# A four-fold folded Fourier transform, and sums and gate products on a second elementwise engine, in a routed attention and long-convolution kernel

## The chip, the cores and the metric

The kernel runs on one core of a Trainium2 chip. The metric is device time in microseconds (us), the median over several executions (a program can also run some per cent slower at a lower clock). "Span" is the length of the one execution that was profiled, which lies about 2 us under the time of the same run. The engines are TensorE (PE in the views, PEld its weight loads), VectorE (DVE), ScalarE (ACT), GpSimd (POOL) and SyncE (SP), which here only issues DMAs; SPq is its queue.

## The reference

```python
def attn(q, k, v, centroids):            # batch 4, 8 heads, 768 rows, 64 columns; 16 centroids a head
    q_assign = argmax(normalised(q) . normalised(centroids))      # likewise k_assign
    mask = q_assign[..., :, None] == k_assign[..., None, :]
    scores = where(mask, q @ k.T / sqrt(64), -1e9)
    p = exp(scores - max);  return (p / (sum(p) + 1e-9)) @ v

def mixer(x, w_proj, filter_fft, w_out): # x: 4 x 768 x 512
    x1, x2, x3 = split(x @ w_proj)
    conv = irfft(rfft(x2) * rfft(filter_fft))      # along the 768 rows
    return (x1 * conv * x3) @ w_out
```

The output of the attention is the input of the mixer. All is float32 outside; inside, scores, spectra and projections are in bfloat16.

## The kernel before

The program is written as some 1,900 small operations, each with the engines that may run it, a duration that the program assumes, and a due time. A planner in the kernel simulates the core at build time with these durations and so fixes the order of every engine's queue. A list of due-time corrections, `NUDGE`, and a dozen settings were tuned so that this plan becomes short.

```python
def op(self, eng, fn, due, r=(), w=(), ...):
    o.eng = eng                        # {"engine": assumed duration in us}
    o.due += NUDGE.get(o.seq, 0.0)     # e.g. {10:3.7, 75:-1.5, 90:7.4, ...}
...
op(("DVE", 1.75), acc, ...)            # probability sum, 128 x 1536
```

The attention takes 96 calls of `pv` (probabilities times values) on TensorE, twelve to a group of four heads; between them stand the scores, the routing of the next group and the mixer of the last finished batch. The spectrum of the mixer is a product with a cosine and sine table `fw`. The rows are first folded once: the sum and the difference of row blocks that mirror each other. So three pairs of products make a spectrum:

```python
def spectrum(ps, i, cs):
    for m in range(3):
        if i < 2:
            columns(ps, T.fw[:, i, m, 192*cs:192*cs+128], T.uv2[:, i, m], m == 0, m == 2)
        ...
```

The spectral sums and the gate products (`y1 * x3`) run on VectorE, save four sums of the last batch.

The softmax here doesn't subtract the row's maximum and nothing guards it: scores larger than these inputs give would overflow.

## Time and profile before

| | kernel before |
|---|---|
| time, median | 389.92 us (388.98 to 390.6, 4 runs) |
| span | 388.5 us |
| TensorE, VectorE, ScalarE, GpSimd busy | 369.0, 359.0, 269.8, 47.0 us |
| first and last `pv` call | start 25.5, end 342.3 us |
| where the plan made at build time ends | 381.2 us |

The prediction below shows the page, the chain and the windows. One view matters besides: what TensorE waits for in its fixed order. Between the 36th and the 96th call (131.3 to 342.3 us) the list of waits has seven rows, 3.1 us in sum, and these lead it. After each pair of waiter and releaser stand us in total, times, and the longest.

```profile
PE bank L73 <- DVE x L871: 0.9, 1, 0.9
PE bank L73 <- DMA aug<-ohT: 0.7, 1, 0.7
```

Waits on VectorE's results make 2.4 of the 3.1 us, masks (`aug<-ohT`) 0.7. The two engines are both almost full, and the order that was found for them makes neither wait for the other.

### The profile page before, as it was taken

To read this page: it belongs to the slowest core of one execution; us is meant where nothing else is said; L and a number is where in the kernel's file an instruction comes from. 1 tells how busy PE (TensorE), PEld (TensorE's weight loads), DVE (VectorE), ACT (ScalarE), POOL (GpSimd) and SP (SyncE) were. 2 spreads that over 40 slices of the span, in tenths; PEclk is the share of its full clock that TensorE was granted. 3 is DMA by queue.
4 is the path that set the end of the run, shared out by engine and by line. 5 is a ranking of instruction groups with operands and counts; after the bars stand their busy time and mean duration, and the time that the engine had idled before them with its cause. 6 is when DMAs were issued, how large, how long until landed. Compare 5 with 4: busy or idle time off the path is not lost.

```text
span 388.5 us, 8482 instructions
## 1 busy us (share of the span) xinstructions
PE 369.0 (95%) x3256; PEld 214.3 (55%) x3256; DVE 359.0 (92%) x509; ACT 269.8 (69%) x514; POOL 47.0 (12%) x92
## 2 busy tenths in 40 slices
PE   2999998999999999999999999999999999999995
PEld 1564454444445555555455554665454566557893
DVE  8898998899899999999899999999999999999782
ACT  5898687887884878787865976778865567632342
POOL 8502000000021010101010100101010100000400
PEclk9999999999999999999999999999999999999999
DMA  9819973740769759966897695745645651110214
GB/s 179 190 52 221 213 165 80 167 120 20 166 134 153 138 83 172 112 144 85 160 136 198 71 275 100 140 88 70 133 60 172 73 161 12 43 43 2 92 74 162
DMA packets 93860, 47.17 MB, mean 121 GB/s; under 512 B 82088, under 2 KB 87676, under 8 KB 93820
## 3 DMA queue, kind: packets, MB, share of 16 engines
q1 hardware_dynamic: 87836, 36.84, 41.6%
q0 software_dynamic: 2704, 8.98, 16.6%
q10 hardware_dynamic: 3280, 0.82, 1.2%
q8 instruction: 25, 0.41, 0.5%
q14 instruction: 15, 0.12, 0.1%
HBM read 31.59 MB, written 7.40 MB: 100 GB/s over the span
## 4 chain that ended last, share of the span: by engine, by line
PE 47%; DVE 35%; issue 7%; ACT 5%; DMA 3%; SPq 0%; DVEq 0%; POOL 0%; ACTq 0%; POOLq 0%
PE bank L73 17%; DVE acc L695 14%; PE pair L681 14%; PE bank L807 5%; PE bank L71 4%; DMA rb<-dr 2%; DVE oh L607 2%; PE bank L555 2%; DVE aug L262 2%; ACT p L670 2%; DVE tm L831 1%; PE bank L584 1%; DVE x L871 1%; ACT aug L260 1%; DVE mx L605 1%
## 5 line engine op out<-in xcount | busy, mean ns | idle before, releaser
L681 PE MATMUL pair<-p,vraw 128*64 128x385 f32 x768 | 142.9, 490 | 0.0
L670 ACT ACTIVATE p<-bank 128x512 f32<-128x512 f32 x192 | 113.7, 610 | 34.8 <-PE bank L73 33.3
L695 DVE TENSOR_TENSOR acc<-p,acc 128x1536 f32<-128x1536 f32 x64 | 111.9, 1749 | 3.5 <-ACT p L670 1.3
L681 PEld LDWEIGHTS pair<-p,vraw 128*64 128x64 f32 x768 | 54.0, 136 | 49.8 <-issue 45.2
L73 PE MATMUL bank<-aug,aug 80*64 80x512 bf16 (+3 forms) x590 | 69.7, 327 | 3.4 <-DVE den L717 1.0
L667 ACT ACTIVATE p<-bank 128x512 f32<-128x512 f32 x96 | 58.6, 610 | 2.7 <-PE bank L73 1.5
L73 PEld LDWEIGHTS <-aug 80*64 80x64 bf16 (+1 forms) x590 | 34.9, 109 | 34.7 <-issue 22.6
L729 POOL DMA_DIRECT2D acc<-acc x30 | 24.0, 799 | 245.5 <-DVE acc L695 85.4
L73 PE MATMUL bank<-xT,wpj 128*64 128x384 bf16 x424 | 41.4, 326 | 0.0
L260 ACT COPY qkT<-bank 128x384 f32<-128x384 f32 x62 | 27.9, 496 | 13.7 <-PE bank L73 8.9
L73 PEld LDWEIGHTS <-wpj 128*64 128x64 bf16 x424 | 27.9, 109 | 12.5 <-issue 6.7
L73 PEld LDWEIGHTS <-y 128*64 128x64 bf16 x448 | 24.9, 110 | 9.1 <-issue 3.0
L695 DVE TENSOR_TENSOR acc<-p,p 128x1536 f32<-128x1536 f32 x16 | 28.0, 1750 | 2.0 <-ACT p L670 2.0
L831 DVE TENSOR_TENSOR tm<-bank,hm 128x512 f32<-128x512 f32 x44 | 27.6, 677 | 0.8 <-ACT p L670 0.5
L260 ACT CAST aug<-qkT 64x768 bf16<-64x768 f32 x29 | 24.0, 829 | 3.0 <-PE bank L73 2.6
L807 PE MATMUL bank<-wpj,xT 128*64 128x512 bf16 x192 | 21.8, 380 | 0.4 <-DVE xT L775 0.4
L73 PE MATMUL bank<-wout,y 128*64 128x512 bf16 x176 | 21.4, 379 | 0.2 <-DVE y L909 0.2
L71 PE MATMUL bank<-aug,aug 80*128 80x256 bf16 (+3 forms) x89 | 19.9, 321 | 0.7 <-DVE tm L831 0.4
L555 PE MATMUL bank<-ident,qkraw 128*128 128x128 f32 x144 | 19.8, 279 | 0.2 <-DVE oh L607 0.2
L555 PEld LDWEIGHTS bank<-ident,qkraw 128*128 128x128 f32 x144 | 15.6, 140 | 7.1 <-issue 5.3
L260 ACT COPY tm<-bank 128x512 f32<-128x512 f32 x14 | 8.1, 590 | 16.1 <-PE bank L807 11.6
L262 DVE CAST aug<-qkT 64x768 bf16<-64x768 f32 x31 | 17.5, 569 | 1.5 <-PE bank L73 0.9
(149 smaller groups left out, 440.6 us busy)
## 6 DMA issues: line engine op xcount, KB each, us to landing
vraw<-in_v_dram SPq DMA_DIRECT2D x16, 384.0 KB, 4.3
qkraw<-in_q_dram SPq DMA_DIRECT2D x30, 192.0 KB, 5.0
qkraw<-in_k_dram SPq DMA_DIRECT2D x30, 192.0 KB, 5.1
rb<-dr SPq DMA_DIRECT2D x30, 192.0 KB, 3.7
out_dram<-ob SPq DMA_DIRECT2D x11, 512.0 KB, 3.6
acc<-acc POOLq DMA_DIRECT2D x10, 384.0 KB, 4.8
acc<-acc POOLq DMA_DIRECT2D x10, 192.0 KB, 4.0
y<-in_moe_filter_fft_dram SPq DMA_DIRECT2D x4, 384.0 KB, 6.8
```

The source lines that it names most:

```text
L71: return T.nc.tensor.matmul(out, lhsT, rhs, start=start, stop=stop)
L73: T.nc.tensor.matmul(out[64 * i:64 * i + 64], lhsT[:, 64 * i:64 * i + 64], rhs, start=start, stop=stop)
L260: T.nc.scalar.copy(out, in_)
L262: (T.nc.vector if e == "DVE" else T.nc.gpsimd).tensor_copy(out, in_)
L555: T.nc.tensor.transpose(bank(h.ids[i // 3])[:, ts(i % 3, 128)], raw(s, i), T.ident)
L667: T.nc.scalar.activation(o, ap(h).rearrange("p (a b) -> p a b", a=2), Act.Exp, scale=0.125)
L670: T.nc.scalar.activation(flat(s)[:, lo:lo + 512], ap(h), Act.Exp, scale=0.125)
L681: T.nc.tensor.matmul(o[64 * hp:64 * hp + 64, ch, :385], T.vraw[vs][:, hp, sk * D:(sk + 1) * D], T.p[slots[sk]][:, hp, 384 * ch:384 * ch + ...
L695: T.nc.vector.tensor_tensor(T.acc[os], P_(t[0]), P_(t[1]) if len(t) == 2 else T.acc[os], op=Alu.add)
L729: op(("POOL", .8), lambda e, rows=rows: T.nc.gpsimd.dma_start(flat_()[:rows], flat_()[rows:2 * rows], accum_op=Alu.add), te, r=[], w=[("ac ...
L807: T.nc.tensor.matmul(ap(h)[64 * i:64 * i + 64], T.xT[xs][:, kt, c:c + 64], T.wpj[:, kt, DM:2 * DM], start=kt == 0, stop=kt == ND - 1)
L831: op(("DVE", .68), lambda e, i=i, cs=cs, r=r, h=h: T.nc.vector.tensor_tensor(T.tm[r][:, cs], ap(h), hmrow(i, (0, 2, 2, 3)[2 * r + cs]), op ...
```

## The change

It folds the rows once more, so that a spectrum takes two pairs of products; two additions over 1024 columns per batch (`quarters`) make the folded rows on VectorE, and half of the query columns are stored in mirrored order so that the rows come out in place. GpSimd may now run the spectral sums and the gate products of all batches but the last. The last batch's gates no longer wait in the inverse's order. The filter comes in 12 transfers of 128 KB, three fp32 products with a flipped identity matrix mirror it, and all settings and the list were fitted anew.

```diff
 def spectrum(ps, i, cs):
-    for m in range(3):
+    for m in range(2):
+        slot = lambda e: T.uv2[:, 4 + (e + cs) % 2 if m else 2 * e + cs]
...
+def quarters(due):
+    for o_, out in ((Alu.add, slice(0, 4, 3)), (Alu.subtract, slice(1, 3))):
+        op(("DVE", 1.2), lambda e, ...: T.nc.vector.tensor_tensor(T.uv2[:, out], T.tm[0], T.tm[1], op=o_), ...)
...
-    op({"POOL": 1.45, "DVE": .68} if last and i < 2 else ("DVE", .68), ...               # spectral sums
+    op({"POOL": 1.45, "DVE": .68} if last and i < 2 or not last else ("DVE", .68), ...
-    op(("DVE", .95), ...                                                                  # gate products
+    op({"DVE": .95, "POOL": 2.2} if not last else ("DVE", .95), ...
-    g = op(("PE", .648), G, ..., after=gs[-1:] + (inv[dt-2:dt-1] if dt > 1 else []))
+    g = op(("PE", .648), G, ..., after=[] if last else gs[-1:] + (inv[dt-2:dt-1] if dt > 1 else []))
...
-LEAD = 1.97516      BUSY = 8.32578      b0 = end - 24.00965      w0 = A(24 * (b + 1)) + 11.85069
+LEAD = 21.93933     BUSY = 20.94041     b0 = end - 40.78980      w0 = A(24 * (b + 1)) + 44.32403
-NUDGE = {10:3.7,75:-1.5,90:7.4, ...}                   # and the other settings
+NUDGE = {2:0.3,3:0.6,5:-0.1, ...}
```

(The settings, one to a line in the program, are gathered here.)

## The prediction

> **What bounds the kernel now.** I read the page first, parts 1 and 2.
>
> ```profile
> PE 369.0 (95%) x3256; PEld 214.3 (55%) x3256; DVE 359.0 (92%) x509; ACT 269.8 (69%) x514; POOL 47.0 (12%) x92
> ...
> PE   2999998999999999999999999999999999999995
> PEld 1564454444445555555455554665454566557893
> DVE  8898998899899999999899999999999999999782
> ```
>
> Two engines look full, so busy time alone does not say which one sets the end. Matmul ends are modelled, so I rebuilt TensorE's work from the chain of waits, where calls stand back to back.
>
> ```profile
> 134.60 1.45 PE pair L681 x8
> 136.04 0.65 PE bank L450 x6
> 136.69 1.30 PE pair L681 x8
> 137.99 0.65 PE bank L450 x6
> ```
>
> One attention-value call (8 instructions) is 1.30 us, or 1.45 just after a change of array shape; a spectrum call of three pairs of 64-row matmuls over 512 columns is 0.65, so 0.217 a pair. In the same view twelve fp32 transposes took 1.46 us, sixteen similarity matmuls 1.43, forty-eight 512-column matmuls 5.23. With these unit costs and the program's order of instructions (0.13 us for each of 82 shape changes) TensorE's work is 363 us: 13 before the first attention-value call, 308 from there to the last, 41 after. The windows cut at those calls:
>
> ```profile
> 0.00:25.50 25.50, 17.43 (x130) 10.93 (x130) 22.21 (x52) 19.20 (x38) 14.46 (x52) 1.00 0.74 156
> 25.50:342.10 316.60, 310.04 (x2623) 169.56 (x2622) 300.94 (x399) 235.10 (x447) 27.54 (x36) 1.00 0.65 125
> 342.10:388.50 46.40, 41.56 (x509) 33.83 (x505) 35.83 (x60) 15.51 (x30) 5.01 (x4) 0.99 0.21 78
> ```
>
> After each length come PE, PEld, DVE, ACT and POOL. The middle holds 308 us of TensorE work in 316.6 us: 8.6 us is all that TensorE loses to anybody in 96 key tiles. VectorE is busy 301 of the 316.6. So TensorE bounds the middle, with VectorE close behind. The start loses 12 us (25.5 less 13), mostly before any data or VectorE's first tables are ready.
>
> The last part I read in the timeline. The last channel mixer starts its 48 projection matmuls at 348.75. Its VectorE work then runs almost without a gap from the first line below until the inverse starts:
>
> ```profile
> 352.95 3.67 DVE L820 TENSOR_TENSOR uv<-tm,bank 128x512 bf16<-128x512 f32 x6
> ...
> 358.97 2.50 POOL L835 TENSOR_TENSOR y<-tm 128x512 bf16<-128x512 f32 x2 [49.60 <-DVE tm L831]
> ...
> 360.28 2.52 DVE L831 TENSOR_TENSOR tm<-bank,hm 128x512 f32<-128x512 f32 x4 [0.27 <-POOL y L835]
> ...
> 368.19 0.72 PE L73 MATMUL bank<-inv,y 128*64 128x192 bf16 x12
> ```
>
> TensorE is kept busy meanwhile with gates and with the third batch's output product, but it is the VectorE chain that releases the inverse at 368.19.
>
> **What the Trainium skill says.** "TensorE: Matmul & The Clock Gate", Back-to-back issue gap, gives 518 cycles for 512 columns, 216 ns; this trace agrees (0.217 a pair). "Perfetto Trace Analysis", Identifying the Most-Contended Engine, says matmul busy share is no good measure of the distance to the roofline; hence the work sum. "GPSIMD Engine Reference", Elementwise side-by-side, has GpSimd about 1.96 times slower on a two-input operation; here the spectral sum is 1272 ns against 676, or 1.88. "SBUF — State Buffer", Who interferes with whom, says that VectorE with two SBUF inputs contends with a GpSimd instruction that reads SBUF, and that one is blocked outright; with one SBUF input it does not. The trace shows both sides: a one-column operation of VectorE took 0.78 us instead of 0.16 and ended when GpSimd's cast did, while the four PSUM-fed products above (360.28) ran at 0.63 each beside two GpSimd sums.
>
> ```profile
> 8.46 0.16 DVE L318 TENSOR_TENSOR s<-s,ss 128x1 f32<-128x1 f32 x1
> ...
> 8.60 0.82 POOL L262 CAST aug<-qkT 64x768 bf16<-64x768 f32 x1
> 8.65 0.78 DVE L319 TENSOR_TENSOR s<-s,s 128x1 f32<-128x1 f32 x1
> ```
>
> **The change, part by part.** The rows of groups that I cost with:
>
> ```profile
> L831 DVE TENSOR_TENSOR tm<-bank,hm 128x512 f32<-128x512 f32 x44 | 27.6, 677 | 0.8 <-ACT p L670 0.5 <-POOL y L835 0.3
> L835 DVE TENSOR_TENSOR y<-tm 128x512 bf16<-128x512 f32 x20 | 13.0, 676 | 0.0
> L909 DVE TENSOR_TENSOR y<-yy,x 128x768 bf16<-128x768 f32 x12 | 11.5, 958 | 0.5
> L835 POOL TENSOR_TENSOR y<-tm 128x512 bf16<-128x512 f32 x4 | 5.0, 1272 | 49.8 <-DVE tm L831 49.8
> L262 DVE CAST aug<-qkT 64x768 bf16<-64x768 f32 x31 | 17.5, 569 | 1.5 <-PE bank L73 0.9
> ```
>
> *TensorE.* Each of 30 spectrum calls (6 in the tables, 24 in the batches) goes from three pairs to two: 30 x 0.217 = 6.5 us removed. Fewer table transposes: 0.4. Added: three fp32 matmuls with the flip matrix; an fp32 pair of 385 columns is 0.325 x 2, so 512 columns are 0.86 each, 2.6 us. Shape changes go from 82 to 78 (0.5). Net -4.8, to 358. By place: -2.9 up to the last attention-value call, -1.9 after it (1.3 of it spectra, the rest a gate call that moves ahead).
>
> *VectorE.* The instruction orders of both kernels count: 17 spectral sums go to GpSimd (17 x 0.676 = 11.5), 9 gate products too (9 x 0.958 = 8.6), 11 casts go to ScalarE (6.3), two table adds of 1536 columns (3.5), one of three angle chains (2.7) and some copies (2.2) vanish. Added: two quarter butterflies over 1024 columns per batch, 1.21 each between the 677 ns of 512 columns and the 1749 of 1536: 9.7; ten table butterflies, 6.8; ten evictions taken from ScalarE, 5.5, and a small copy. Net -12.6, to 346. In the last batch, though, the butterflies are +2.4 in the chain that releases the inverse.
>
> *GpSimd.* +17 x 1.272 = 21.6, and 9 products over 768 columns, estimated from 1272 ns at 1.9 us each: 17. It ends near 85 us. Where VectorE's next instruction has two SBUF inputs, as the 1.75 us sum of the probabilities has, it waits. At an estimated 0.3 to 0.5 us for each of 26 moves, 8 to 13 us of VectorE's gain is handed back, as waiting or longer instructions. *ScalarE* gains some 6 us; with 69% busy that costs nothing.
>
> **What lies on the path.** Middle: TensorE -2.9. VectorE's relief lies beside it and can only cut into the 8.6 us of stalls; the port waits and GpSimd's queue, where sums stand behind the accumulating DMAs, add some. I take -0.5 net. Start: with one angle chain fewer, VectorE's centroid part and so the first scores come earlier; I take -1.5 of 2.7. End: TensorE has 1.9 less to do, but the inverse waits for VectorE. Its work from the first butterfly to the last sum was 15.2 us; it becomes about 18 (quarters +2.4, more gate products ahead of the inverse +1.5, the rest -1), and TensorE's fill is 5.2 + 10.4 + 2.6 + 3.5 = 21.7 us with all gates ahead of the inverse against 19.4 before. After the inverse's start four gate products fewer stand in the way. The two nearly cancel: -0.8. Sum: -2.9 - 0.5 - 1.5 - 0.8 = -5.7, and 389.7 becomes 384.0.
>
> **Rivals.** (a) VectorE was the real bound, and its 12.6 us count nearly in full: for it, the long stretches of probability sums in the chain of waits (35% VectorE); against it, only 8.6 us of stall in the middle. That gives about 379. (b) The port lock and the queue behind the DMAs eat the relief, and VectorE becomes the bound with some 355 us and new gaps; TensorE's saving turns to idle time. For it: the blocked operation above and 26 moves onto an engine that was idle; against it: the sums are followed mostly by PSUM-fed products. That gives 386 to 390. (c) The end grows, since the butterflies lengthen its only chain: +1 to +2 there, so about 386.
>
> **Range and chances.** Faster by over 2% means under 381.9, which needs at least 2 us of the stalls gone besides all that I counted: 0.27. The schedule's many tuned priorities could give that, or take it. Slower by over 2% would need over 12 us of new waiting (7.8 and the 4.8 saved), more than the middle loses now: 0.03. Range 379.5 to 388.0.
>
> **What would show it.** Right: TensorE's busy time near 364, VectorE's at 346 to 352 with probability sums or table adds that last over 1.75 us beside GpSimd's sums; the last attention-value call 4 to 6 us earlier than 342; the distance from the last projection's start to the end about unchanged at 39.7. Wrong: a first attention-value call still at 25.5; stalls in the middle well under 8.6 (rival a), or VectorE waiting for GpSimd by more than 5 us in sum (b); a longer end (c).

## More of the kernel before

The filter comes in four transfers of 384 KB, and the routing of each group ends in a transposing DMA from SyncE, followed by eight small transfers (the masks) into the operands of the scores:

```python
op(("SP", .6), lambda e: T.nc.sync.dma_start_transpose(T.ohT..., T.oh...), due - 2, r=both("oh"), ...)
masks(n, range(2), due + 1.3)
```

## The result, and the profile after

The changed kernel takes **406.14 us** (403.88 to 408.92, 4 runs), against 389.92. Ratios here and below compare fast runs of the same rounds, so they are not quite the ratio of the medians quoted. This one is 1.0421, with a 95% interval of 1.0352 to 1.049. The kernel is slower by 4%, where the prediction had it 1.5% faster. The page of the changed kernel, parts 1 and 2:

```profile
PE 370.7 (92%) x3274; PEld 214.6 (53%) x3274; DVE 361.9 (89%) x491; ACT 276.9 (68%) x518; POOL 90.3 (22%) x117
...
PE   3999189999999998999898999999898999999995
...
DVE  8789639899899789999997899999999999999981
```

VectorE does as much as before (359.0), although 26 operations went to GpSimd. In the fifth of the forty slices, at 40 to 50 us, TensorE stands almost still. The windows, cut at the first and last `pv` call, show that the loss lies between the two:

```profile
26.18:359.00 332.82, 311.58 (x2646) 174.61 (x2647) 305.62 (x381) 241.96 (x451) 69.86 (x61) 0.98 0.61 119
359.00:404.70 45.70, 39.98 (x499) 27.32 (x495) 35.24 (x58) 15.80 (x30) 6.86 (x5) 0.99 0.21 79
```

The middle grew from 316.6 to 332.8 us; the end hardly moved (46.4 to 45.7).

To find where in the middle, I added up TensorE's work in program order with the unit costs of the prediction and took it from the time at which every twelfth `pv` call ended. What is left is TensorE's lost time so far. (The last two columns are experiments, told below.)

| `pv` calls | before | changed | filters in a row | planned anew |
|---|---|---|---|---|
| 12 | 14.2 | 24.1 | 13.6 | 12.8 |
| 36 | 17.0 | 24.5 | 14.0 | 13.6 |
| 48 | 18.1 | 29.6 | 19.2 | 15.0 |
| 60 | 19.3 | 34.0 | 24.3 | 17.5 |
| 96 | 20.8 | 40.4 | 30.7 | 18.5 |
| end | 25.8 | 46.8 | 37.2 | 24.4 |

There are two losses: some 10 us before the twelfth call, and from the 36th call on some 16 us where the kernel before loses 4. The end costs both kernels 5 to 6.5.

**The first loss.** SyncE's queue in the changed kernel (start, length, operation, output<-input, count; timeline):

```profile
27.07 6.34 SPq L388 DMA_DIRECT2D y<-in_moe_filter_fft_dram  x10
36.96 1.53 SPq L659 DMA_TRANSPOSE ohT<-oh  x1
38.54 1.26 SPq L388 DMA_DIRECT2D y<-in_moe_filter_fft_dram  x2
```

Ten of the twelve filter transfers go out, then a transposing DMA stands in the queue until VectorE has finished the routing it reads, at 36.9 us. The other two filter transfers stand behind it. Meanwhile GpSimd, whose guard waits for one filter piece alone, has started the 2 MB of weights at 35.5 us. The two late pieces, 128 KB each, land at 51.5 us, and TensorE waits for them:

```profile
51.66 2.04 PE L432 MATMUL bank<-y,xT 128*128 128x512 f32 x2 [7.49 <-DMA y<-in_moe_filter_fft_dram]
```

The wait is 7.5 us of the loss. Some 2 us more come after it, as the windows around it show; after the busy times stand the clock that was granted to TensorE (1.00 is full speed), the DMA share and GB/s:

```profile
44.00:51.00 7.00, 0.17 (x1) 0.00 (x0) 2.73 (x5) 0.00 (x0) 0.00 (x0) 0.85 1.17 199
51.00:55.00 4.00, 3.34 (x11) 0.85 (x11) 1.25 (x3) 0.60 (x1) 0.00 (x0) 0.50 1.05 233
55.00:57.00 2.00, 2.00 (x14) 0.74 (x12) 1.70 (x2) 0.49 (x1) 0.00 (x0) 0.82 0.12 39
57.00:61.00 4.00, 4.00 (x38) 2.06 (x35) 1.09 (x2) 2.68 (x5) 0.00 (x0) 1.00 0.74 169
```

The two matmuls above took 2.04 us at half the clock; in e2 below, where TensorE does not stand still, the same two took 1.02. The estimate from these windows is 3.34 x 0.5 + 2.00 x 0.18, or 2 us.

**VectorE's lengthening.** The durations (least, median, largest, in ns) of the large sums of VectorE in the kernel before, then in the changed one, where the next two lines are GpSimd's sums and products:

```profile
L695 DVE TENSOR_TENSOR acc<-p,acc x64: 1694/1752/1759, 28.7 to 342.0; 128x1536 f32<-128x1536 f32 x64
```

```profile
L727 DVE TENSOR_TENSOR acc<-p,acc x64: 1695/1757/3520, 30.1 to 359.1; 128x1536 f32<-128x1536 f32 x64
...
L869 POOL TENSOR_TENSOR y<-tm x21: 1262/1273/2716, 163.8 to 382.5; 128x512 bf16<-128x512 f32 x21
L944 POOL TENSOR_TENSOR y<-yy,x x9: 1815/1819/3180, 189.5 to 362.0; 128x768 bf16<-128x768 f32 x9
```

The medians agree, the largest do not: some instructions were held for most of another one's length, on either side. From the groups' means, the lengthening on VectorE is 64 x (1813 - 1749) = 4.1 us for these, 16 x (1938 - 1750) = 3.0 for the other large sums, 10 x (642 - 173) = 4.7 for an operation over 12 columns, and 15 x (1165 - 1006) = 2.4 for the normalised output: 14.2 us.

### The profile page after: what moved, and what is told of

The parts are those of the page before. It is cut to its first block, busy times and chain, and to the rows that moved or that the text cites. A ratio compares the mean times of both kernels' runs of the same rounds, so it can differ in the third digit from the quotient of the medians.

```text
span 404.7 us, 8563 instructions
## 1 busy us (share of the span) xinstructions
PE 370.7 (92%) x3274; PEld 214.6 (53%) x3274; DVE 361.9 (89%) x491; ACT 276.9 (68%) x518; POOL 90.3 (22%) x117
## 4 chain that ended last, share of the span: by engine, by line
PE 45%; DVE 25%; DMA 9%; ACT 8%; issue 7%; SPq 4%; ACTq 0%; DVEq 0%; POOL 0%; POOLq 0%
PE bank L74 18%; PE pair L713 13%; DVE acc L727 6%; SPq L492 3%; DMA y<-in_moe_filter_fft_dram 3%; PE bank L839 3%; ACT aug L267 2%; ACT p L702 2%; DVE oh L639 2%; DMA ohT<-oh 2%; DMA rb<-dr 2%; DVE tm L865 2%; PE bank L72 1%; PE bank L586 1%; DVE xT L807 1%
## 5 line engine op out<-in xcount | busy, mean ns | idle before, releaser
L702 ACT ACTIVATE p<-bank 128x512 f32<-128x512 f32 x192 | 113.0, 609 | 37.4 <-PE bank L74 24.3
L727 DVE TENSOR_TENSOR acc<-p,acc 128x1536 f32<-128x1536 f32 x64 | 116.1, 1813 | 3.4 <-ACT p L702 1.2
L74 PE MATMUL bank<-aug,aug 80*64 80x512 bf16 (+3 forms) x616 | 73.4, 329 | 6.0 <-DMA aug<-ohT 1.6
L74 PE MATMUL bank<-xT,wpj 128*64 128x384 bf16 x488 | 46.9, 326 | 0.4 <-DVE oh L639 0.4
L869 POOL TENSOR_TENSOR y<-tm 128x512 bf16<-128x512 f32 x21 | 31.9, 1527 | 39.5 <-DVE tm L865 25.0
L74 PEld LDWEIGHTS <-wpj 128*64 128x64 bf16 x488 | 31.9, 109 | 14.5 <-issue 7.1
L267 ACT CAST aug<-qkT 64x768 bf16<-64x768 f32 x41 | 33.6, 829 | 2.3 <-DVE qkT L269 1.0
L727 DVE TENSOR_TENSOR acc<-p,p 128x1536 f32<-128x1536 f32 x16 | 31.0, 1938 | 1.5 <-DMA dd<-acc 0.9
L944 POOL TENSOR_TENSOR y<-yy,x 128x768 bf16<-128x768 f32 x9 | 18.3, 2032 | 35.5 <-DVE yy L941 27.1
L586 PE MATMUL bank<-ident,qkraw 128*128 128x128 f32 x144 | 19.2, 279 | 0.3 <-DVE x L906 0.3
L267 ACT COPY ob<-bank 128x512 f32<-128x512 f32 x22 | 12.7, 589 | 9.5 <-PE bank L74 9.0
L72 PE MATMUL bank<-aug,aug 128*128 128x256 bf16 (+3 forms) x76 | 16.8, 321 | 1.5 <-DMA aug<-ohT 0.7
## 6 DMA issues: line engine op xcount, KB each, us to landing
vraw<-in_v_dram SPq DMA_DIRECT2D x16, 384.0 KB, 4.2
acc<-acc POOLq DMA_DIRECT2D x10, 384.0 KB, 5.1
```

The source lines that it names most:

```text
L72: return T.nc.tensor.matmul(out, lhsT, rhs, start=start, stop=stop)
L74: T.nc.tensor.matmul(out[64 * i:64 * i + 64], lhsT[:, 64 * i:64 * i + 64], rhs, start=start, stop=stop)
L267: T.nc.scalar.copy(out, in_)
L586: T.nc.tensor.transpose(bank(h.ids[i // 3])[:, ts(i % 3, 128)], raw(s, i), T.ident)
L702: T.nc.scalar.activation(flat(s)[:, lo:lo + 512], ap(h), Act.Exp, scale=0.125)
L727: T.nc.vector.tensor_tensor(T.acc[os], P_(t[0]), P_(t[1]) if len(t) == 2 else T.acc[os], op=Alu.add)
```

## The experiments

All kernels are correct unless stated, and every ratio is to the kernel before in the same rounds.

**Theories at the start.** A: the filter loads behind the transposing DMA cost the first 9 to 10 us. B: GpSimd's sums and products cost the rest. C: the fitted settings, above all `LEAD`, which lets loads go out early, cost the rest.

### e1: the twelve filter loads in a row

```diff
+    first = min(order.index(o) for o in T.early)       # T.early: the twelve filter loads
+    order = [o for o in order[:first] if o not in T.early] + T.early + [o for o in order[first:] if o not in T.early]
```

> Theory A (a filter load stuck in a queue): in the changed kernel the last two of twelve filter loads stand on SyncE's queue behind a transposing DMA that waits for VectorE until 36.96; they then share the DMA engines with 2 MB of weights and land only at 51.5, while TensorE waits in order at the third flip product. With the twelve loads issued in a row, all else in the same order, the wait of 7.5 us goes and the time falls by 8 to 11 us from 406 to about 396. Rival (the stall only covers waits that would come later anyway, since VectorE and the masks are late): under 3 us, 403 or more.

Measured: 397.11 us, ratio 1.0155 (1.0108 to 1.0203). That is 9.0 us below the changed kernel, and theory A is shown. The second loss is all there, as the table shows (14.0 at call 36, 30.7 at call 96). From here on e1 is the base.

### e2: the weights held until the last filter piece

```diff
-        op(("POOL", .1), lambda e: T.nc.gpsimd.tensor_copy(T.wpj[0:1, :, 0:1], T.f[1][0:1, 0, 0:4]...), 29,
+        def gate(e):
+            for r in (0, 64):
+                T.nc.gpsimd.tensor_copy(T.wpj[r:r + 1, :, 0:1], T.f[1][r:r + 1, 2, 0:4]...)
+        op(("POOL", .1), gate, 29,
```

> Order of the queues as in the changed kernel, but the 2 MB of weight loads start only when the last filter piece has landed. If it is the sharing with the weights that stretches the two late loads to 12.3 us (theory A2), they land in about 3 to 5 us after their issue at 38.5 and the time falls by some 6 to 8 us, to about 399. If the place in SyncE's queue alone is to blame (rival), they still land late and the time stays within 2 us of 406.

Measured: 398.76 us, ratio 1.0197. With the queue as it was, keeping the weights back takes 7.4 us from the changed kernel's time. In the trace the whole first loss is gone: TensorE waits for no filter piece, and its 36th `pv` call ends at 122.0 us, in e1 at 122.2. So the first loss is two small transfers sharing the way with 2 MB; their late issue alone costs nothing that can be seen. The 1.6 us by which e2 trails e1 are within the noise (give or take 2.8 us, from the intervals of the two ratios), and in the traces they arise after call 36, where the waits for masks, explained under e9, sum to 5.7 us against 4.2.

### e3: the sums and products back on VectorE

```diff
+    for o in T.moved:          # the 17 sums and 9 products of batches 0 to 2 (e1 as the base)
+        o.on = "DVE"
```

> As e1_filter_first, but the 17 spectral sums and 9 gate products that went to GpSimd run on VectorE again, at the same place in the program's order. Theory B (GpSimd gives back what it takes): VectorE's instructions with two SBUF inputs [...] lost about 14 us to longer durations in the changed kernel (sums of probabilities 1813 and 1938 ns against 1749, the small column operation 642 against 173, the scaled copy to xT 1165 against 1006), while 20 us of work left it, so moving back changes VectorE's busy time by only +4 to +7 and the time by -3 to +4 us against e1. Rival 1 (GpSimd was a clear gain): slower than e1 by over 5 us. Rival 2 (GpSimd is the main loss): faster than e1 by over 4 us.

Measured: 398.67 us, ratio 1.0193, 1.6 us above e1. The lengthening is gone:

```profile
L727 DVE TENSOR_TENSOR acc<-p,acc x64: 1696/1757/1761, 28.6 to 350.9; 128x1536 f32<-128x1536 f32 x64
```

VectorE's busy time is 365.2 us against 361.6. Moving 26 operations to GpSimd takes some 20 us from VectorE and gives most of it back as held instructions; the net is 3.6 us of VectorE. The 1.6 us of time are not clear of noise (give or take 2.6). Theory B falls, as undoing the move does not make e1 faster: in this order the move is not what costs.

### e4: the old LEAD

```diff
-LEAD = 21.93933
+LEAD = 1.97516        # e1 as the base
```

> As e1_filter_first, but the lead of loads (how long before its due time a load may be issued) is 1.98 again instead of 21.94, and the scheduler plans anew. Theory C (early loads of q, k and v crowd the queue and the DMA engines in front of the routing masks, whose transposing DMA landed in a median of 13.2 us instead of 2.8): the masks land in 3 to 6 us again and the time falls by another 3 to 6 us below e1, to about 391. Rival (the long lead is not what delays the masks, and the other tuned priorities fit the long lead): no gain, within 2 us of e1 or slower.

Measured: 406.08 us, ratio 1.039, 9 us slower than e1. Theory C in this form falls, but the run says little more: the planner makes a wholly new order with a list that was fitted to the other setting, and its own plan ends at 389.4 us, 10.8 later than with the new `LEAD`.

### e5 to e8: what the mixed stage is worth to each engine

e5 makes the quarter additions short. Its output is wrong, which doesn't matter for the time.

```diff
-T.nc.vector.tensor_tensor(T.uv2[:, out], T.tm[0], T.tm[1], op=o_)
+T.nc.vector.tensor_tensor(T.uv2[:, out, :16], T.tm[0][:, :, :16], T.tm[1][:, :, :16], op=o_)
```

> Wrong on purpose (not correct): with the filter loads in a row as in e1_filter_first, and each of the eight quarter additions (1222 ns each on VectorE in the changed kernel) over 16 of its 512 columns. It takes about 8 x 1.2 = 9 us of work from VectorE, alone, and leaves TensorE, GpSimd and every order as they are. Theory D (VectorE sets the pace of the mixed stage, from call 36 of the 96 attention-value calls on): 6 to 9 us below e1 (397.1), 388 to 391. Rival E (TensorE's work or the late routing masks set it): no more than 2 us below e1.

e6b gives TensorE its third pair back, once thrown away.

```diff
-        for m in range(2):
+        for m, first, final in ((0, True, True), (0, True, False), (1, False, True)):
```

> The result stays right: e1 with the first pair of products of each of the 30 spectrum calls issued twice (once thrown away), which gives TensorE back the third pair that the change took out: 30 x 0.217 = 6.5 us, 24 of them in the mixed stage (5.2). Theory D: TensorE has slack there, so at most 2 us above e1. Rival E (TensorE bounds it, as the prediction had it): 5 to 6.5 us above e1.

Measured, page part 1 of e5 and then of e6b:

```profile
PE 365.1 (94%) x3274; PEld 209.0 (54%) x3274; DVE 353.7 (91%) x491; ACT 276.7 (71%) x518; POOL 90.1 (23%) x117
```

```profile
PE 372.5 (93%) x3334; PEld 214.5 (54%) x3334; DVE 362.1 (91%) x491; ACT 276.5 (69%) x518; POOL 89.9 (23%) x117
```

e5 took 394.91 us, ratio 1.0071 (1.0004 to 1.0139): with 7.9 us of VectorE less (361.6 to 353.7), 0.0084 of 390, or 3.3 us, are won, give or take 3.2. e6b took 399.49 us, ratio 1.0206 (1.0147 to 1.0265): with 6.2 us of TensorE more, 0.0051 of 390, or 2.0 us, are lost, give or take 3.0. e5 lies between what the two theories expected, e6b at the upper edge of theory D. What can be said is that in this order neither engine's work counts one to one; the shares, two fifths and a third, are rough.

One thing moves between these runs that no edit aimed at: TensorE's waits for masks sum to 4.2 us in e1's profiled run, 5.5 in e3's, 1.6 in e5's (391.59 us, the fastest of its four by 3 us) and 3.9 in e6b's, with SyncE's queue in the same order. A difference of 1 or 2 us between two of them is therefore not to be read as the effect of the edit.

e7 moves the query, key and value loads near a transposing DMA behind its masks:

```diff
+    for tr, ms in T.routes:       # a transposing DMA and its eight masks
+        late = [loads within 6 us before tr, or between tr and the last mask]
+        order = [... all but late, up to the last mask ...] + late + [... the rest ...]
```

> e1 with the loads of query, key and value that stand in SyncE's queue just before or between a transposing DMA of the routing and its mask transfers moved behind the masks; nothing else moves. Theory F (late masks, held up by queue and bandwidth, cost a part of the mixed stage): the attention-value calls 36 to 60 come 3 to 6 us earlier and the end with them. Rival (VectorE holds the stage anyway, theory D): within 1 us of e1.

Measured: 402.83 us, ratio 1.0297, slower than e1. What the edit aimed at came: the transposing DMA that in e1 is issued at 113.0 us, and followed by its first mask 8.5 us later, is here followed by it after 2.8. But TensorE now waited 5.0 us in two waits for copies of queries and keys that came late. The edit was too coarse, and it leaves theory F open.

e8 chains the last gates again:

```diff
-  after=[] if last else gs[-1:] + (inv[dt - 2:dt - 1] if dt > 1 else []))
+  after=gs[-1:] + (inv[dt - 2:dt - 1] if dt > 1 else []))
```

> e1 with the last batch's gates chained in the inverse's order again, as in the kernel before; only the orders of TensorE and VectorE in the last projection, transform and output differ. The prediction gave this part 0.8 us. If it was right, 0.5 to 1.5 us above e1; the stretch from the start of the last projection to the end, 39.8 us in before and in the changed kernel, suggests within 0.5 us.

Measured: 397.78 us, ratio 1.0148 beside e1's 1.0155. The ratios put it 0.3 us below e1, give or take 3.2, the medians 0.7 above; that cannot tell nothing from the predicted 0.8. In the profiled runs (e8's is its slowest) the stretch from the start of the last projection to the end of the last matmul is 36.2 us here and 35.3 in e1, and to the end of the span 43.0 and 40.0. So what the separated gates are worth stays open.

### e9: masks that wait for nothing

e1's list of TensorE's waits between the 36th and the 96th call (122.2 to 349.3 us) sums to 12.5 us, where that of the kernel before had 3.1. Its first five rows:

```profile
PE bank L74 <- DMA aug<-ohT: 2.6, 2, 1.5
PE bank L74 <- DVE x L906: 1.7, 4, 0.8
PE bank L72 <- DMA aug<-ohT: 1.6, 1, 1.6
PE bank L74 <- DVE uv L853: 1.5, 2, 1.2
PE bank L74 <- DVE tm L865: 1.5, 4, 0.7
```

Late masks make 4.2 us, and results of VectorE, spread over nine rows, 8.3. For e9 the transposing DMAs are taken from the order, and the masks copy old rows. Its output is wrong, which doesn't matter for the time.

```diff
+    order = [o for o in order if o not in T.gone]           # the seven transposing DMAs
-    rows = slice(64*j + 2*pr + hp, 64*j + 64, 4) if n else slice(64*pr + 32*j + 16*hp, ...)
+    rows = slice(64 + 32*j + 16*hp, 64 + 32*j + 16*hp + 16)
```

> Wrong on purpose: e1 with the seven transposing DMAs of the routing taken out of the emitted order and every mask transfer reading rows that the first batch wrote. Orders of all engines stay, only SyncE's queue loses the seven. In e1, TensorE waited 4.2 us for routing masks between call 36 and call 96 and 8.3 us for results of VectorE. Theory F (the masks cost what is waited for them): 3 to 5 us below e1 (397.1), 392 to 394. Theory D (VectorE holds the mixed stage): the wait moves to VectorE's results, at most 2 us below e1. Either way the waits on masks must be gone from the trace.

Measured: 393.09 us, ratio 1.0069; no wait on masks is left in the list. Theory F holds for its part: of the 6 us by which e1 trails the kernel before, about 3.4 (0.0086 of 390, give or take 2.1) are masks. The transposing DMA that e1 issues at 113.0 us, with loads of queries, keys and values around it in the queue, is followed by its first mask after 8.5 us; in the kernel before none takes more than 5.4. e7 shows that these loads delay it (2.8 us without them). That the large `LEAD` is what put them there was not shown.

### e10 and e11: both kernels without their fitted lists

```diff
-NUDGE = {...}
+NUDGE = {}
```

> The kernel before with its list of hand-fitted priorities emptied, everything else its own. At build time its planner then plans an end at 395.8 us (381.2 with the list; the chip took 389.9, 8.7 more). Theory G (the plan's durations are nearly right for the kernel before, whatever the order): 403 to 407 us, that is 7 to 11 above its plan. Rival H (the gap to the plan is an accident of one order): gap anywhere from 5 to 25.

> e1 with its list of priorities emptied, its other settings kept. Its planner plans 386.1 us (378.6 with the list; e1 took 397.1 on the chip, 18.5 more). Theory G (the changed kernel runs further behind any plan, because GpSimd's additions lengthen VectorE's, which the plan does not know, and its masks land later than planned): 402 to 408, 16 to 22 above its plan, so no faster than the kernel before without its list. Rival H (the extra 10 us are an accident of e1's one fitted order): 394 to 397, 8 to 11 above its plan, and clearly faster than the kernel before without its list.

Measured: before without its list 404.05 us (ratio 1.0353), changed with the filters in a row and without its list 397.13 (1.0161). Without lists the changed kernel is 7 us faster. The two should not be read as a clean measure of the change: the kernel before without its list loses only after the last `pv` call, which ends at 342.0 us there and at 342.3 with the list. But the gap to the plan tells something. Times are the medians:

| kernel | plan ends | measured | gap | VectorE too short in the plan |
|---|---|---|---|---|
| before | 381.2 | 389.9 | 8.7 | 22.8 |
| before, no list (e10) | 395.8 | 404.1 | 8.3 | 23.3 |
| changed, filters in a row (e1) | 378.6 | 397.1 | 18.5 | 34.9 |
| the same, old `LEAD` (e4) | 389.4 | 406.1 | 16.7 | 28.2 |
| the same, no list (e11) | 386.1 | 397.1 | 11.0 | 27.5 |
| changed, planned anew (e12) | 382.5 | 384.5 | 2.0 | 7.7 |
| before, planned anew (e13) | 381.2 | 388.5 | 7.3 | 13.2 |

The last column is the busy time of VectorE in the trace less what the planner of that kernel counts for it (it can be run again from the kernel's file). The gap grows with it by and large, but the plan of the kernel before, too, had VectorE 23 us too short and was off by only 8.7.

The list of the kernel before is worth 14.6 us in the plan and 14.1 on the chip. The changed kernel's is worth 7.5 in the plan and nothing on the chip. Theory G was too pessimistic (11.0 against 16 to 22), and rival H, that this one fitted order is at fault, holds for the larger part.

### e12: the changed kernel planned with measured durations

The plan gives VectorE 326.7 us of work; the trace shows 361.6. To see what this does, I kept e1's order on every engine and computed its times again with durations from e1's trace. All of them together (large sums 1.836 us for 1.75, the two row-sum instructions 1.1 for 0.5, the marking of the largest similarity 1.02 for 0.55, the normalised output 1.17 for 1.05, and a longer transposing DMA, which is an allowance and not a measured size) move the end by 17.0 us, to 395.6. The measured span is 395.1. Taken alone, the transposing DMA moves it most, by some 8 us, then the marking and the large sums. The same for the kernel before, with its own two wrong durations, ends at 387.7; its span is 388.5. This is a calculation, made after the fact, and no run. The run that follows from it puts these durations into the planner and searches the list and the settings anew (by random changes kept if the plan gets shorter, 45 minutes):

```diff
-  op(("DVE", 1.75), acc, ...          op(("DVE", .5), gather, ...       op(("DVE", .55), ... Alu.is_equal
+  op(("DVE", 1.83), acc, ...          op(("DVE", 1.1), gather, ...      op(("DVE", 1.02), ... Alu.is_equal
-  .6 if last else 1.05      "POOL": 1.45 / 2.2     transposing DMA byts=196e3     filter loads due 16.0
+  .6 if last else 1.17      "POOL": 1.55 / 2.1     transposing DMA byts=500e3     filter loads due -20.0
-NUDGE = {...}      LEAD = 21.93933     BUSY = 20.94041    ...
+NUDGE = {...}      LEAD = 21.833338    BUSY = 80.193759   ...
```

> The changed kernel, computing the same, with the durations in its planner set to what the trace of e1 shows (probability sum 1.83 us for 1.75, marking of the largest similarity 1.02 for 0.55, the two row-sum instructions together 1.1 for 0.5, normalised output 1.17 for 1.05, GpSimd's sum 1.55 and product 2.1, a longer transposing DMA, the filter loads first), and its priorities and settings searched anew against that plan, which then ends at 382.5 us. Replaying e1's order with these durations ends at 395.6 (on the chip its span was 395.1), the order of the kernel before with its own measured ones at 387.7 (chip 388.5). Theory J (the changed kernel lost because its fixed orders were planned with too short VectorE work and DMA): 383 to 388, at or below the kernel before. Rival D (VectorE's 362 us and the port hold it at 395 or so in any order): 393 to 398.

Measured: **384.46 us** (384.26 to 385.53, 6 runs), ratio 0.9837 (0.9806 to 0.9867). Same computation, same operations, in another order and a few of them on other engines: 12.7 us faster than e1 and 1.6% faster than the kernel before. Page part 1:

```profile
PE 366.9 (96%) x3241; PEld 212.2 (55%) x3241; DVE 346.7 (91%) x475; ACT 285.2 (74%) x530; POOL 94.9 (25%) x121
```

and the list of TensorE's waits between calls 36 and 96, which has five rows, 2.5 us in sum, led by

```profile
PE bank L72 <- ACT p L702: 0.8, 1, 0.8
PE bank L74 <- DVE oh L639: 0.6, 1, 0.6
PE bank L74 <- DVE x L906: 0.5, 2, 0.3
```

No wait for a mask is left. VectorE's busy time fell by 14.9 us. Some 6 of these are instructions that were lengthened less (7.9 us in sum for 14.1, by the groups' means as above); the rest is optional work that the planner, which now knew how long VectorE takes, moved off it, mostly to ScalarE (277.0 to 285.2) and GpSimd (90.1 to 94.9). So this run does not separate better timing from less VectorE work; both came from the corrected durations and the new search. Nor does it separate the durations from the search: a new search with the old durations was not run.

### e13 and e14: the same search for the kernel before

To be fair the kernel before needs the same search. Its planner got 1.03 us for 0.55 and 0.66 for 0.5, and a new list and settings; e14 is e12's kernel again, on the same chip as e13.

```diff
-  op(("DVE", .5), gather, ...      op(("DVE", .55), ... Alu.is_equal      NUDGE = {...}
+  op(("DVE", .66), gather, ...     op(("DVE", 1.03), ... Alu.is_equal     NUDGE = {...}
```

> The kernel before, computing the same, with two durations of its planner set to what its trace shows (marking of the largest similarity 1.03 us for 0.55, the row-sum instructions 0.66 for 0.5) and its priorities and settings searched anew as long as for e12_refitted; its plan then ends at 381.2 us. If the change is worth its TensorE work once both orders fit (about 5 us, theory J in full): 388 to 391 here, no better than the kernel before. If a better fitted order is worth as much to the kernel before as to the changed one (theory K: e12's gain is the search, the change is worth nothing or little): 381 to 385.

> The kernel of e12_refitted once more, on the same chip as e13_before_refitted: 383 to 386 us. Theory J: 4 us or more below e13; theory K: within 2 us of it.

Measured: e13 388.47 us, ratio 0.9951 (0.9924 to 0.9978); e14 384.28 us, ratio 0.9846 (0.982 to 0.9872). Page part 1 of e13:

```profile
PE 368.1 (95%) x3287; PEld 219.9 (57%) x3287; DVE 356.6 (92%) x505; ACT 275.2 (71%) x520; POOL 45.4 (12%) x90
```

With orders searched alike, the changed kernel is 4.2 us faster, and TensorE's work by the prediction's unit costs is 362.7 against 358.6, 4.1 less. Theory J holds in the main, K does not. That 4.2 and 4.1 agree does not show that TensorE's work is the cause, for VectorE's busy time fell as well, from 356.6 to 348.3 us in e14. Two more reservations: each kernel had one search, and how far two searches of one kernel differ was not tried, so 4.2 us holds for these two orders. And e13's plan is still 7.3 us from the chip and e12's 2.0, so the model of the kernel before is the less exact one, and a better one might narrow the 4.2.

## Why the prediction was wrong

The prediction was 384.0 us in a range of 379.5 to 388.0, and the kernel took 406.1.

**The step that failed** is the one on the path through the middle: "I take -0.5 net", that is, that the 8.6 us which TensorE loses there would stay or shrink. The loss at the last `pv` call grew from 20.8 to 40.4 us, nearly all of it after the first call. The runs put in its place:

- *A stall of 9 to 10 us that the prediction did not have at all.* Two filter loads stood behind a transposing DMA that waited for VectorE, and then shared the way with the weights (e1 -9.0, e2 -7.4 us). The wait was 7.5 us, and about 2 more were lost at the lower clock after it. The Trainium skill, "DMA: Bandwidth & Descriptors", Anatomy of one DMA — SWDGE (gpsimd) path, describes DMAs that GpSimd issues, but says of DMA engines in general that they do not wait on semaphores and that any such wait happens on the issuing sequencer before dispatch; the queue above shows it for SyncE, two ready loads held to 38.54 us by one wait that ended at 36.9. The split could have been read blind, as the order of SyncE's queue shows the filter loads ten and two; I followed the compute engines' orders only.
- *Some 13 us in the mixed stage, where the order did not fit the machine.* By the table e1 loses 16.7 us from call 36 to the last where the kernel before loses 3.8. It lost 3.0 less before call 36 and loses 1.5 more at the end, so 11.4 more in all; the 4.8 us of TensorE work saved leave 6.6 of it, and that is the difference of the spans (395.1 and 388.5). In the lists of waits the masks are 3.5 us more than before (4.2 and 0.7), and e9 wins about 3.4 without them. Results of VectorE are 5.9 more (8.3 and 2.4), at places where the plan, which had VectorE 35 us too short, saw none. Some 3.5 us of the 13 stand in no list. That new durations and a new search together remove the loss is shown by e12. That the short durations caused it is argued, from the calculation and the table of gaps; it is not shown by a run.

**Where work was taken for time.** The prediction made TensorE the bound and counted its -2.9 us one to one. In e1's order 6.2 us more of TensorE cost 2.0, give or take 3.0 (e6b), and 7.9 us less of VectorE won 3.3, give or take 3.2 (e5): both less than one to one.

**VectorE's sum.** The terms were right and the estimate of the lock a little low. Quarter additions were predicted at 1.21 us and took 1.22; GpSimd's sums and products were taken as 1272 ns and 1.9 us and have undisturbed medians of 1273 and 1819 ns. The lengthening was 14.2 us where 8 to 13 was estimated. With it 346 becomes some 360; the trace has 361.9. The prediction's own sign for being right, 346 to 352, did not fit its sum: with the 8 to 13 us that it had handed back it should have said 354 to 359. The Trainium skill, "SBUF — State Buffer", Who interferes with whom, says that whoever comes second is blocked for the whole instruction, and counts the operation of a tensor with a constant (`tensor_scalar`) among those that can take the shared pair of ports. The trace agrees: a sum held to 3520 ns, and such an operation, the addition of a constant over 12 columns, at 642 ns on average for 173 (174 in e3, where the moved work is back). It is rival (b) in its first half; its second half, GpSimd's queue holding VectorE up, did not come, as e1's VectorE waits 1.0 us for GpSimd's sums after call 36.

**The start.** "I take -1.5" failed: the first `pv` call began at 26.1 us in the changed kernel and at 25.3 in e1, against 25.5. One angle chain fewer bought nothing there.

**The end.** -0.8 was predicted, and nothing came. From the start of the last projection to the end it is 39.75 us before, 39.9 in the changed kernel and 40.0 in e1. What the separated gates alone are worth, e8 could not tell. The text that the two "nearly cancel" was right, rival (c) did not come.

**The work sum was right.** TensorE's busy time was to be near 364; it is 366.3 in e1, 366.9 in e12 and 370.7 in the changed kernel with its stalls and its stretch at a lower clock. One reading in it was loose: the 216 ns that it takes from the skill stand there for an isolated matmul, and for a stream the page gives less, while the trace's 0.217 is of calls that stand back to back. What the change is worth when the order fits was predicted as 5.7 us and measured as 4.2 (e13 to e14). That these are near is in part luck, for the terms are not: in the two traces the first `pv` call starts at the same time (25.3 and 25.4 us, where -1.5 was predicted), the stretch from there to the last is 5.2 us shorter (predicted -3.4), and what follows is 1.8 longer (predicted -0.8). The arithmetic "slower by over 2% would need over 12 us of new waiting" was right too. Its 3% was wrong, because it asked what the edit adds, and the new waiting came from all orders having been made anew. The sentence that the tuned priorities "could give that, or take it" deserved to be the largest term of the range.

## What to carry to other kernels

When a change re-plans a fixed schedule, predict the work and the order apart: read the queue of every issuing engine for loads that now stand behind a wait, and widen the range by what the old tuning was worth (14 us here). A schedule fitted against assumed durations is only as good as these; compare the busy time that the plan assumes with that of the trace before trusting it, correct it, and fit again. When two engines are both over 90% busy, test what each is worth by padding and shortening it: here neither counted one to one.

## What the Trainium skill lacked or had wrong

- "SBUF — State Buffer": it says that one side is blocked outright, but beside ratios for single pairs of instructions it gives no price for a stream of interleaved ones. Here 26 operations moved to GpSimd made VectorE's own instructions 14.2 us longer in sum, about 0.55 us for each one moved, and of some 20 us moved only 3.6 us of VectorE's busy time were left, and no gain in time clear of noise (e3: 1.6 us, give or take 2.6).
- "Perfetto Trace Analysis": optimising the engine with the highest occupancy first does not say what a microsecond of it is worth when a second one is as full. Here 6.2 us more of TensorE cost 2.0, give or take 3.0, and 7.9 us less of VectorE won 3.3, give or take 3.2.
- No page has it: how far a schedule fixed at build time may drift from the chip. With assumed durations that made VectorE 35 us too short, the changed kernel ran 18.5 us behind its plan (e1); with measured ones and a new search, 2.0 (e12). The kernel before, with 23 us too short, ran 8.7 behind.
- "DMA: Bandwidth & Descriptors": it has the wait on the issuing sequencer, but no figure for how much a small load is stretched by a large one that shares the engines. Two loads of 128 KB issued at 38.5 us beside 2 MB of weights landed at 51.5; with the weights held back, TensorE had them by 42.95 (e2).
